# Low-rank token mix after a gated linear recurrence on one Trainium2 core: V r as one float32r product per chunk of stacked halves, and one pair fewer on split weights

## The chip, the cores and the metric

The kernel runs on one core of one Trainium2 chip. The metric is the device time of one execution in microseconds (us); three runs of the kernel before took 533.96, 535.43 and 535.63, a median of 535.43.

A core has engines that run side by side, each through its own queue of instructions in order: PE multiplies matrices (PEld is its loading of weights), DVE and ACT do elementwise work, POOL some of it, and SP issues most of the DMAs. An instruction that waits on a semaphore holds all that is queued behind it on its engine.

## What is computed

Inputs are q, k, v and a complex gate a of shape (4, 8, 768, 48): four batches, eight heads, 768 tokens, 48 columns. The reference first runs a linear recurrence over the tokens of each head, and then a mixer on x of shape (4, 768, 384):

```python
for t in range(S):
    ar, ai = (a_re_n[:, :, t, :, None], a_im_n[:, :, t, :, None])
    new_re = ar * S_re - ai * S_im
    new_im = ar * S_im + ai * S_re
    kv = np.einsum('bhd,bhe->bhde', k[:, :, t], v[:, :, t])
    S_re, S_im = (new_re + kv, new_im)
    y[:, :, t] = np.einsum('bhd,bhde->bhe', q[:, :, t], S_re)
...
    xt = x.transpose(0, 2, 1)
    h = xt @ U @ V
    u = x + h.transpose(0, 2, 1)
    ch = np.maximum(u @ w_ch1, 0.0) @ w_ch2
    return (u + ch).astype(np.float32)
```

Here a_re_n, a_im_n is the gate with its magnitude limited to 0.999. U is 768x32, V 32x768, w_ch1 (w1 below) 384x1536 and w_ch2 (w2) 1536x384. The product x^T U, here called r, is 384x32 in each batch; V r below is what is added to x.

## The kernel before

**Tiles and stages.** The tokens of a batch are six chunks of 128. For each group of two chunks, `gates` makes the decay factors on DVE, ACT and PE; `prep` and `chain` compute the chunk's recurrence with matrix products on PE and leave the chunk's 128x384 of x in a tile `xo`. Two chunks make a pair: three pairs to a batch, twelve in all, numbered 0 to 11. `mixer(m)` does the channel part of pair m:

- `rank` (L1003), once in each batch when its last chunk is there: U^T x for all six chunks, summed in one bank. Four groups of 32 partitions hold r's 32 rows for four column groups, 96 columns each, so r is a tile of 128x96. ACT copies it to SBUF (L1009).
- `spread` (L1063): V r of the pair in eight float32 products (two chunks by four column groups, 32 rows of contraction each), into four banks.
- `mixed` (L467, 128x192): four additions on DVE give u = x + V r in place of `xo`.
- `turned` (L1082): u is transposed on PE for the next product. For pairs 1 to 11 it is then split: DVE takes the upper bits (low, L1104), ACT makes uh (L1106), DVE the rest ul (L1107) and the sum ud (L1109).
- `cut_weights` (L1124 to L1136), once, in pair 1: the same splitting of w1, in six parts of 128x768. DVE masks (wt, L1124), subtracts (w, L1126) and makes wd (L1130); ACT makes wl (L461) and wh (L1136).
- `up_cut` (L1148, L1150, L1155), pairs 1 to 11: u w1 as three float32r products, uh·wh, ul·wl and ud·wd, 36 of each in a pair, 128x256. ACT takes the first two out of PSUM (L461), and DVE adds the third and applies the relu (h, L1169).
- `up` (L1179): the same as one plain float32 product, 36 in a pair. Pair 0 uses it, before V r is known, on x alone ("ahead"). `ranked` (L1190 to L1200) takes r through w1 and `corrected` (L1214 on PE, h L1220 on DVE) then adds V (r w1) to what `up` made.
- the second product, h w2: `down` plain for pair 0 (L1243, 128x384), `down_two` (L1286, 128x192) for pairs 1 to 8, `down_three` (L1463) for the rest.

**Weights.** `weights` and `single` load w1, U, V and w2 and put each together from the two 32-bit words of a number (loads L602, DVE and ACT L616 to L622 and L467; tiles `stage`, `w`). V lies in SBUF as one tile of 128 partitions, its 32 rows four times, one copy for each column group.

**Order.** Every instruction group is an operation in a plan. A table of numbers, `ORDER`, fixes one common order for all engines; each engine's queue is that order cut to its own operations. Nothing is decided later: an engine takes its next instruction when its semaphores are there. `SPARE` says ahead of which operations PE gets idle products of the identity (53 of them). DMAs are issued on SP in the same order; there are transfers of q, k, v (192 KB, L581 and L583), of the gate (L574), of w2 (`stage`, 768 KB, L602), and for each chunk a small trip through DRAM and back (TD<-es L765, T<-TD L768) that turns a row.

## Time and profile before

| | |
|---|---|
| runs | 533.96, 535.43, 535.63 us; median 535.43 |
| the profiled execution | 535.18 us, its span 533.3 |
| granted TensorE clock | 1.00 |
| V r, L1063 | 8.4 us busy in 192 records |
| cut products L1148, L1150, L1155 | 70.6, 68.5 and 55.2 us busy, 396 records each |
| plain up L1179 | 17.4 us busy in 72 records |
| HBM | 33.60 MB read, 4.76 MB written |

The span runs from the first to the last recorded instruction; 1.9 us of the execution's time lie around it. Busy times of PE count each matmul until its modelled end, so neighbours overlap and the mean of a group is longer than the step from one to the next. A group's row reads: line, engine, operation, out<-in by the names of the tiles, shape, count, then busy us, mean ns of one, and the idle time of the engine just before, with what ended it.

### The profile page before, as it was taken

To read this page: it belongs to the slowest core of one execution; us is meant where nothing else is said; L and a number is where in the kernel's file an instruction comes from. 1 tells how busy PE (TensorE), PEld (TensorE's weight loads), DVE (VectorE), ACT (ScalarE), POOL (GpSimd) and SP (SyncE) were. 2 spreads that over 40 slices of the span, in tenths; PEclk is the share of its full clock that TensorE was granted. 3 is DMA by queue.
4 is the path that set the end of the run, shared out by engine and by line. 5 is a ranking of instruction groups with operands and counts; after the bars stand their busy time and mean duration, and the time that the engine had idled before them with its cause. 6 is when DMAs were issued, how large, how long until landed. Compare 5 with 4: busy or idle time off the path is not lost.

```text
span 533.3 us, 17003 instructions
## 1 busy us (share of the span) xinstructions
PE 511.0 (96%) x7454; PEld 466.5 (87%) x7454; DVE 430.7 (81%) x798; ACT 310.5 (58%) x554; POOL 29.9 (6%) x57
## 2 busy tenths in 40 slices
PE   7789999899999998999999999999999999999996
PEld 7567686469999988999999989999999899999996
DVE  7998999999998976886977866786967758788741
ACT  6879999777587783655568764453475652321000
POOL 1000000000102000011002000011002000000020
PEclk9999999999999999999999999999999999999999
DMA  9996968430254442303217460024104300000011
GB/s 185 206 214 163 225 166 197 87 60 1 39 85 105 92 97 29 61 30 69 45 32 128 79 121 17 16 40 91 31 3 85 62 12 2 1 1 1 0 64 52
DMA packets 150704, 39.92 MB, mean 75 GB/s; under 512 B 145880, under 2 KB 147440, under 8 KB 150624
## 3 DMA queue, kind: packets, MB, share of 16 engines
q1 hardware_dynamic: 148544, 34.63, 33.1%
q0 software_dynamic: 2080, 4.15, 2.3%
q8 instruction: 59, 0.97, 0.8%
q14 instruction: 21, 0.17, 0.1%
HBM read 33.60 MB, written 4.76 MB: 72 GB/s over the span
## 4 chain that ended last, share of the span: by engine, by line
PE 79%; DVE 10%; ACT 6%; issue 2%; DMA 1%; SPq 0%; ACTq 0%; DVEq 0%
PE down L1286 20%; PE up L1148 8%; PE bank L1155 8%; PE up L1150 8%; PE bank L1463 7%; PE bank L910 4%; PE bank L881 4%; PE bank L968 4%; PE bank L930 3%; PE bank L960 3%; PE down L1243 2%; PE up L1179 2%; PE bank L1063 1%; PE bank L814 1%; DMA qk<-in_q_dram 1%
## 5 line engine op out<-in xcount | busy, mean ns | idle before, releaser
L1148 PE MATMUL up<-uh,wh 128*128 128x256 f32 x396 | 70.6, 287 | 0.1
L1150 PE MATMUL up<-ul,wl 128*128 128x256 f32 x396 | 68.5, 281 | 0.3 <-DVE ul L1107 0.3
L461 ACT ACTIVATE h<-up 128x512 f32<-128x512 f32 x60 | 35.2, 594 | 46.8 <-PE up L1150 46.3
L1148 PEld LDWEIGHTS up<-uh,wh 128*128 128x128 f32 x396 | 56.8, 189 | 1.2 <-ACT h L461 0.3
L1150 PEld LDWEIGHTS up<-ul,wl 128*128 128x128 f32 x396 | 56.2, 189 | 0.5 <-DVE ul L1107 0.5
L887 ACT COPY QK<-bank 112x512 f32<-112x512 f32 x96 | 51.2, 590 | 8.8 <-PE bank L881 8.6
L1155 PE MATMUL bank<-ud,wd 128*128 128x256 f32 x396 | 55.2, 283 | 0.0
L1286 PE MATMUL down<-w,h 128*128 128x192 f32 x288 | 53.6, 331 | 0.2
L1155 PEld LDWEIGHTS bank<-ud,wd 128*128 128x128 f32 x396 | 50.7, 188 | 0.2
L464 DVE TENSOR_TENSOR QKC<-qk,cs 128x768 f32<-128x768 f32 x48 | 44.9, 955 | 5.8 <-ACT cs L461 4.0
L1286 PEld LDWEIGHTS down<-w,h 128*128 128x128 f32 x288 | 46.6, 190 | 1.5 <-DVE h L1169 0.4
L467 DVE TENSOR_TENSOR xo<-bank,xo 128x192 f32<-128x192 f32 x78 | 26.1, 354 | 24.3 <-PE bank L1463 17.5
L1169 DVE CUSTOM_DVE_ANT_0 h<-bank,h 128x512 f32<-128x512 f32 x54 | 35.8, 687 | 10.2 <-PE bank L1155 8.1
L1286 PE MATMUL down<-stage 128*128 128x192 f32 x192 | 35.7, 333 | 0.5 <-issue 0.3
L800 POOL DMA_DIRECT2D z<-F x15 | 12.1, 806 | 376.1 <-ACT z L461 102.9
L1286 PEld LDWEIGHTS down<-stage 128*128 128x128 f32 x192 | 31.0, 190 | 1.6 <-issue 0.4
L458 ACT ACT_TABLE_LOAD x24 | 30.8, 1283 | 1.1 <-PEq L1670 0.7
L881 PE MATMUL bank<-ident,QKC 64*112 64x64 f32 x768 | 28.5, 220 | 2.4 <-DVE QKC L464 1.7
L881 PEld LDWEIGHTS bank<-ident,QKC 64*112 64x112 f32 x768 | 24.1, 130 | 7.5 <-issue 2.6
L1106 ACT CAST uh<-low 128x384 fp32r<-128x384 f32 x22 | 11.2, 509 | 31.2 <-DVE low L1104 26.6
L910 PE MATMUL bank<-QK 112*64 112x64 f32 x768 | 27.6, 225 | 0.6 <-ACT QK L887 0.6
L910 PEld LDWEIGHTS bank<-QK 112*64 112x64 f32 x768 | 24.3, 138 | 3.9 <-issue 1.7
(234 smaller groups left out, 1066.4 us busy)
## 6 DMA issues: line engine op xcount, KB each, us to landing
stage<-in_moe_w_ch_dram SPq DMA_DIRECT2D x12, 768.0 KB
qk<-in_q_dram SPq DMA_DIRECT2D x24, 192.0 KB
qk<-in_k_dram SPq DMA_DIRECT2D x24, 192.0 KB
values<-in_v_dram SPq DMA_DIRECT2D x24, 192.0 KB
gate<-in_a_re_dram SPq DMA_DIRECT2D x22, 192.0 KB
gate<-in_a_im_dram SPq DMA_DIRECT2D x22, 192.0 KB
out_dram<-xo POOLq DMA_DIRECT2D x13, 192.0 KB, 3.0
out_dram<-xo POOLq DMA_DIRECT2D x16, 96.0 KB, 3.1
```

The source lines that it names most:

```text
L458: ACT(1.4, rank, lambda: nc.scalar.preload_act_table_set(name), writes=[TABLE])
L461: return nc.scalar.activation(out=o, in_=i, func=f, **kw)
L464: nc.vector.tensor_tensor(out=o, in0=a, in1=b, op=OP.mult)
L881: nc.tensor.transpose(out=get(*ps[r])[0:DQ, h], in_=get(*qkc)[at, h].rearrange("p u d -> p (u d)")[:, 0:DQ], identity=ident[at, at], tile_ ...
L887: nc.scalar.copy(out=get(*QK)[0:DQ, u].rearrange("p (h t) -> p h t", t=CH)[:, :, r * HC:(r + 1) * HC], in_=get(*ps[r])[0:DQ])
L910: nc.tensor.matmul(out=get(*ps0)[r:r + HC, h], lhsT=k_of(h, r, HC), rhs=q_of(h, r, HC), start=True, stop=True, tile_position=(0, r))
L1148: nc.tensor.matmul(out=get(*X)[:, e], lhsT=get("wh", f)[:, at(e)], rhs=get(*uh)[:, f], start=(f == 0), stop=False)
L1150: nc.tensor.matmul(out=get(*X)[:, e], lhsT=wl_of(f)[:, at(e)], rhs=get(*ul)[:, f], start=False, stop=(f == KD - 1))
L1155: nc.tensor.matmul(out=get(*Y)[:, e], lhsT=wd[:, f, at(e)], rhs=get(*ud)[:, f], start=(f == 0), stop=(f == KD - 1))
L1169: DVE(c_dve(2 * N), R0, lambda: nc.vector._custom_dve(dve_ops.TENSOR_ADD_SAT, out=where_(), in0=get(*Y), in1=where_(), s0=math.inf, s1=0.0 ...
L1286: nc.tensor.matmul(out=get(*to)[:, part], lhsT=x(j), rhs=y[:, j], start=(first and j == 0), stop=(j == KH - 1), skip_group_check=not first)
L1463: nc.tensor.matmul(out=get(*ps), lhsT=w[0]()[:, q], rhs=x[0]()[:, q], start=(n == 0 and q == 0), stop=(q == k3 - 1), skip_group_check=True)
```

## The change

1. **Pair 1 goes plain.** A new number CUTS = 2 says from which pair on the up product is split. Pair 1 uses `up` (L1179, 36 more float32 products, ACT applies the relu), and u is copied, not split. `cut_weights` is called in pair 2.
2. **V r from stacked halves.** V4 holds V's four copies in float32r: rounded by ACT, and in the second and fourth group of 32 partitions the remainder V − rounded V (two subtractions on DVE). R4, 128x384, holds r's 32 rows four times: rounded in the first and second group, the remainder in the third and fourth. So the four combinations of upper and lower halves are summed by one product 128x384 with 128 rows of contraction: one for each chunk, 24 in all, instead of eight for each pair. `mixed` adds two tiles of 128x384 instead of four of 128x192.
3. **How R4 comes about.** r (128x96, now kept in the first columns of `prefix_z`) is written to DRAM (RD) by a DMA on SP and loaded back into `low`, four times 32x384. In batch 0, where column groups interleave, these are 12 DMAs of 32x4x32; in batches 1 to 3, with another grouping of columns (`thirds_of`), four of 32x4x96. ACT rounds `low` into R4, and DVE subtracts in the lower 64 partitions.
4. **Storage.** The last third of wd shares a buffer with V, which is free once pair 0's corrections are done; QKC lies without gaps; five constants share a tile. w1's two parts get their names by EDGES, with the same borders.
5. **Order.** ORDER and SPARE are new tables; the idle products are 79 instead of 53, the added ones ahead of early operations.

```diff
     PLAIN = 1
     THREE = 9
-    SINGLE, AHEAD = 3, 1
+    SINGLE, AHEAD, CUTS = 3, 1, 2
...
-    wd = singles.tile([128, KD, FF], FR, name="wd")
+    wd = singles.tile([128, KD - 1, FF], FR, name="wd")
+    buffer(("V", 0), "last", 1, [128, S], padded=[128, FF])
+    buffer(("wdx", 0), "last", 1, [128, FF], dtype=FR)
+
+    def wd_of(f):
+        return wd[:, f] if f < KD - 1 else get("wdx", 0)
...
-    V = singles.tile([128, S], FP, name="V")
...
+    V4 = singles.tile([128, S], FR, name="V4")
+    R4 = singles.tile([128, DM], FR, name="R4")
...
+                    ACT(c_act(S), ("w1", p), lambda: nc.scalar.copy(out=V4, in_=get("V", 0)), [("V", 0)], [("V4", 0)])
+                    for n in range(1, NP, 2):
+                        at = slice(n * R, (n + 1) * R)
+                        DVE(c_dve(S), ("w1", p), lambda at=at: nc.vector.tensor_tensor(
+                            out=V4[at], in0=get("V", 0)[at], in1=V4[at].bitcast(FP), op=OP.subtract), [("V", 0)], [("V4", 0, at.start)])
...
-            buffer(r, "r", 1, [128, RC])
+            ring(r, "r", [prefix_z[:, 0:RC]])
...
-                                         rhs=quarter_of(get("xo", b * NCH + c), n), start=(c == 0), stop=(c == NCH - 1),
+                                         rhs=(thirds_of if b else quarter_of)(get("xo", b * NCH + c), n), start=(c == 0), stop=(c == NCH - 1),
...
-            ACT(c_act(RC), R0, lambda: nc.scalar.copy(out=get(*r), in_=get(*sums_r)), [sums_r], [r])
+            ACT(c_act(RC), R0, lambda: nc.scalar.copy(out=get(*r), in_=get(*sums_r)), [sums_r], [r] + [("prefix_z", 0)] * (b == 0))
+            rd = ("RD", b)
+            buffer(rd, "RD", 2, [128, RC], bass.MemoryType.DRAM)
+            SP(0.3, ("load", 7), lambda: nc.sync.dma_start(out=get(*rd), in_=get(*r)), [r], [rd])
+            for n in range(NP):
+                def spread_r(n=n):
+                    x = get(*rd).rearrange("(n r) c -> r n c", r=R)
+                    o = low[n * R:(n + 1) * R]
+                    if b:
+                        nc.sync.dma_start(out=o.rearrange("r (n c) -> r n c", n=NP), in_=x)
+                    else:
+                        for f in range(KD):
+                            nc.sync.dma_start(out=o[:, f * 128:(f + 1) * 128].rearrange("r (n t) -> r n t", t=R), in_=x[:, :, f * R:(f + 1) * R])
+                SP(0.3, ("load", 7), spread_r, [rd], [("low", 0, n)])
+            ACT(c_act(DM), R0, lambda: nc.scalar.copy(out=R4, in_=low), [("low", 0)], [("R4", 0)])
+            DVE(c_dve(DM), R0, lambda: nc.vector.tensor_tensor(
+                out=R4[2 * R:], in0=low[2 * R:], in1=R4[2 * R:].bitcast(FP), op=OP.subtract), [("low", 0)], [("R4", 0)])
...
-                if m == AHEAD:
+                if m == CUTS:
...
-            ps = [out_of("mixed", (m, n), [128, MC, RC], [128, 512 // RC // MC * MC, RC]) for n in range(NP)]
-
-            def products():
-                for cc in range(MC):
-                    for n in range(NP):
-                        at, c = slice(n * R, (n + 1) * R), c0 + cc
-                        nc.tensor.matmul(out=get(*ps[n])[:, cc], lhsT=V[at, c * CH:(c + 1) * CH],
-                                         rhs=get(*r)[at], start=True, stop=True, tile_position=(n * R, 0))
-            PE(0.45, R0, products, [r, ("V", 0)], ps, way=4, steps=4 * NP)
+            ps = [out_of("mixed", (m, cc), [128, DM], [128, 512]) for cc in range(MC)]
+            for cc in range(MC):
+                at = slice((c0 + cc) * CH, (c0 + cc + 1) * CH)
+                PE(0.18, R0, lambda cc=cc, at=at: nc.tensor.matmul(out=get(*ps[cc]), lhsT=V4[:, at], rhs=R4, start=True, stop=True),
+                   [("R4", 0), ("V4", 0)], [ps[cc]], steps=1)
             return ps
 
-        def mixed(n, ps):
-            u = XO[i0 // MC % len(XO)].rearrange("p c (f n t) -> p n c f t", n=NP, t=R)[:, n]
-            DVE(c_dve(MC * RC), R0, lambda: add(u, get(*ps)[:, 0:MC].rearrange("p c (f t) -> p c f t", t=R), u), [ps],
-                [("xo", i0 + cc) for cc in range(MC)])
+        def mixed(cc, ps):
+            DVE(c_dve(DM), R0, lambda: add(get("xo", i0 + cc), get(*ps), get("xo", i0 + cc)), [ps], [("xo", i0 + cc)])
...
-            if ahead:
+            if m < CUTS:
                 for r in range(2):
                     def keep(copy, r=r):
...
-        if m >= AHEAD:
-            if m == AHEAD:
+        if AHEAD <= m < CUTS:
+            for ff in range(0, KF, 2):
+                up(ff)
+        if m >= CUTS:
+            if m == CUTS:
                 cut_weights()
             for ff in range(0, KF, 2):
                 up_cut(ff)

```

The remaining edits rename what point 4 says. The first lines of the tables (the numbers count operations of two different plans):

```diff
-    92, 113, 95, 114, 115, 94, 116, 117, 2206, 0, 93, 97, 91, 3, 96, 118, 4, 98, 99, 102, 103, 104, 119, 105, 106, 120, 121, 107, 108, 110, 112, 111,
+    95, 2202, 98, 97, 116, 117, 118, 119, 120, 121, 96, 94, 193, 0, 5, 151, 99, 100, 122, 123, 101, 102, 105, 106, 107, 103, 108, 109, 3, 124, 110, 4,
```

Three places of the new order, with the lines of the kernel that each row stands in (before and after count lines apart: L1027 is the rank product after, L1100 the new V r product, L1211 up, L1229 the product of r and w1, L1247 corrected, L1253 its sum, L1276 down).

PE, before, from the rank product of batch 0 (up is a piece of pair 0's up product, bank_62<-r,V the first of the eight V r products):

```order
L1003 MATMUL rank<-xo_134,UV 32x96 x8
L1179 MATMUL up<-uT,w_138 128x256
L1179 MATMUL up<-uT,w_139 128x256
L1179 MATMUL up<-uT,w_140 128x256
L1063 MATMUL bank_62<-r,V 128x96
```

PE, after, at the first V r product (the rank product stands some twenty rows ahead of these; R_102 is R4, V_101 is V4, bank_63<-GS and zs belong to the gates of a later group):

```order
L1247 MATMUL bank_66<-V,stage 128x256
L1247 MATMUL bank_61<-V,stage 128x256
L1276 MATMUL down<-w_99,h 128x384 x6
L1100 MATMUL bank_62<-R_102,V_101 128x384
L834 MATMUL bank_63<-GS_115,prefix_r 128x384
L834 MATMUL bank_63<-zs_1419,prefix_r 128x384
L1276 MATMUL down<-w_99,h 128x384 x4
L1100 MATMUL bank_64<-R_102,V_101 128x384
```

Before, V r follows the rank product with one piece of up between; after, it stands behind the corrections and the first six down products.

DVE, before, at the sums of the corrections (w_138 and w_139 are parts of w1, wt the cut):

```order
L467 TENSOR_TENSOR xo_133<-bank_65,xo_133 128x6x32
L622 TENSOR_SCALAR w_96<-w_96 128x768
L1126 TENSOR_TENSOR w_138<-w_138,wt 128x768 x2
L1126 TENSOR_TENSOR w_139<-w_139,wt 128x768
L1220 ISA h<-bank_63,h 128x256
L1220 ISA h<-bank_65,h 128x2x256
L808 CAST GS_115<-z 128x384
L1220 ISA h<-bank_66,h 128x2x256
L1220 ISA h<-bank_61,h 128x2x256
```

DVE, after, at the same sums (F, stage, GS and w_99 belong to gates and weights, R_102<-low,R_102 is R4's subtraction):

```order
L1253 ISA h<-bank_64,h 128x2x256
L1253 ISA h<-bank_65,h 128x2x256
L1253 ISA h<-bank_62,h 128x256
L634 TENSOR_SCALAR w_99<-w_99 128x768
L1048 TENSOR_TENSOR R_102<-low,R_102 64x384
L1253 ISA h<-bank_66,h 128x256
L828 CAST GS_115<-z 128x384
L829 TENSOR_TENSOR zs_1419<-z,GS_115 128x384
L634 TENSOR_SCALAR w_99<-w_99 128x768
```

The cuts of w1 (L1126 before) are gone from here; the subtraction for R4 stands between the sums.

SP, after, around r's write in batch 0 (prefix_z holds r; gate, qk and stage are loads from the inputs):

```order
L586 DMA gate<-in_a_im_dram 128x8x48
L593 DMA qk<-in_k_dram 128x8x48
L1036 DMA RD<-prefix_z 128x96
L614 DMA stage<-in_moe_w_ch_dram 128x2x768
L1045 DMA low<-RD 32x4x32 x3
L586 DMA gate<-in_a_im_dram 128x8x48
L1045 DMA low<-RD 32x4x32 x3
L586 DMA gate<-in_a_re_dram 128x8x48
L785 DMA TD<-es 1x384
L1045 DMA low<-RD 32x4x32 x6
L595 DMA values<-in_v_dram 128x8x48 x2
```

The write and the loads of r take their turns among the loads of the inputs; before there is no transfer of r.

## The prediction

> **What bounds the kernel now.** I read the page first, for the engines and for the chain that ended last.

> ```profile
> span 533.3 us, 17003 instructions
> PE 511.0 (96%) x7454; PEld 466.5 (87%) x7454; DVE 430.7 (81%) x798; ACT 310.5 (58%) x554; POOL 29.9 (6%) x57
> PE 79%; DVE 10%; ACT 6%; issue 2%; DMA 1%; SPq 0%; ACTq 0%; DVEq 0%
> ```

> PE is busy for 96% of the span and carries 79% of the chain; the 10% on DVE must lie somewhere. The windows (busy us of PE, PEld, DVE, ACT, POOL in a stretch, then the granted clock, the DMA share and GB/s) say where:

> ```profile
> 0.00:10.00 10.00, 8.19 (x58) 8.00 (x58) 7.13 (x23) 4.83 (x9) 1.68 (x13) 1.00 0.87 191
> 90.00:100.00 10.00, 6.97 (x42) 3.65 (x39) 10.00 (x19) 9.60 (x14) 0.79 (x1) 1.00 0.99 199
> 100.00:140.00 40.00, 39.38 (x321) 31.52 (x320) 39.60 (x68) 25.29 (x40) 1.68 (x3) 1.00 0.15 26
> 204.00:500.00 296.00, 294.04 (x4216) 281.95 (x4209) 228.49 (x425) 148.94 (x275) 18.66 (x29) 1.00 0.22 42
> ```

> From 204 to 500 us PE lacks 1.96 us of 296: there only PE work counts. From 90 to 140 us DVE has 0.4 us of slack in 50, and PE loses 3.03 us in one slice, 90 to 100, where the DMA engines also stand at 0.99. The chain of waits (start, us, what) through that place:

> ```profile
> 84.83 0.37 PE rank L1003 x8
> 85.20 1.49 PE up L1179 x6
> 86.70 0.67 PE bank L1063 x16
> ...
> 87.62 0.55 DVE wt L1124
> ...
> 90.80 2.60 DVE w L1126 x3
> 93.40 0.93 DVE h L1220 x2
> ...
> 98.17 0.70 PE bank L1214 x4
> ```

> The rank product of batch 0 ends at 85.2, V r follows at 86.7, and DVE cuts w1 (L1124, L1126) before it comes to the corrected h (L1220) for which PE waits. These are PE's longest waits from 84 to 116 us (in all, times, longest):

> ```profile
> PE bank L1214 <- DVE h L1220: 1.4, 1, 1.4
> PE down L1243 <- DVE h L1220: 1.1, 1, 1.1
> ```

> **The change, part by part: PE work.** Paces come from unbroken pieces of the chain, where start to start is what counts. A float32 matmul leaves two records, so L1179 x12 is six matmuls and L1063 x16 eight.

> ```profile
> 63.81 2.59 PE up L1179 x12
> ...
> 103.77 2.58 PE down L1243 x8
> 106.35 0.35 PE bank L814 x2
> ...
> 109.28 0.56 PE bank L1082 x12
> ...
> 205.05 0.25 ACT r L1009
> ...
> 205.34 0.70 PE bank L1063 x16
> 206.04 0.55 PE bank L814 x2
> ...
> 208.09 0.63 PE bank L1063 x16
> ...
> 242.60 0.72 PE bank L1155 x6
> ```

> A plain up product takes 2.59/6 = 0.432 us, a cut product 0.72/6 = 0.12. Pair 1 trades 3×36 cut products (108×0.12 = 13.0 us) for 36 plain ones (15.5 us): **+2.5**. V r costs 0.63 a pair, 7.6 us over 12 pairs. The nearest rows to one float32r product of 128x384 are L814's, of the same shape on float32r data, at 0.175 or 0.275 a piece: 24 make 4.2 to 6.6 us, a saving of 1.0 to 3.4. I take 0.2, nearer the quick pair, which stands between down products as most of the new ones do: **−2.8**. PE work comes out at −0.3, bounds −0.9 and +1.5. The added idle matmuls of the first 10 us go into its 1.8 us without work: 0; without that cover, 26 of them at the 0.43 us of the larger up product would be 11 us at most, but PE has nothing else queued there.

> **DVE.** Rows of its groups (busy, mean ns). Back to back, a duration holds 0.09 us that the next one overlaps (L464 gives 0.955, and L1126 of the same size 2.60/3 = 0.87 on the chain above).

> ```profile
> L467 DVE TENSOR_TENSOR xo<-bank,xo 128x192 f32<-128x192 f32 x78 | 26.1, 354 | 24.3 <-PE bank L1463 17.5 <-PE bank L1063 4.6 <-issue 2.1
> L1169 DVE CUSTOM_DVE_ANT_0 h<-bank,h 128x512 f32<-128x512 f32 x54 | 35.8, 687 | 10.2 <-PE bank L1155 8.1 <-ACT h L461 1.2 <-ACT cs L461 0.8
> L1104 DVE TENSOR_SCALAR low<-bank 128x384 uint32<-128x384 uint32 x22 | 12.2, 555 | 7.0 <-ACT uh L1106 4.5 <-PE bank L1082 2.6
> L464 DVE TENSOR_TENSOR QKC<-qk,cs 128x768 f32<-128x768 f32 x48 | 44.9, 955 | 5.8 <-ACT cs L461 4.0 <-PE bank L881 1.7
> ```

> The sums that add V r to x go from four of 128x192 to two of 128x384 (L1104's size): 4×0.26−2×0.47 = 0.1 us a pair, hidden where PE alone counts. Pair 1 loses six h sums (6×0.60) and the cutting of u (two low and two ul of 0.47, one ud of 0.86): 6.3 us. The cuts of w1 move behind L1220: 0.55+2.60 = 3.15 us leave the stretch of the chain above, while two subtractions for V4 (768 long, so 0.87 each by L464) and one for R4 (384 long, 0.47) come in: L1220 could start 3.15−1.74 = 1.4 us earlier, and end some 3 us earlier where two cuts (L1130, of L464's size) stood between its last instructions. That can give at most PE's 3.03 us of 90 to 100.

> **The exchange.** Where V r waited for one copy by ACT, r now goes to DRAM and back before R4 exists. No row of before has such a trip. These stand nearest: the longest transfer on the chain, a small one of POOL's queue (median to landing), and SP's longest wait for the small write of its own DRAM trip:

> ```profile
> 53.07 5.71 DMA qk<-in_q_dram
> ```

> ```profile
> z<-F POOLq DMA_DIRECT2D x15, 1.5 KB, 1.9
> ```

> ```profile
> SPq L768 <- DMA TD<-es: 7.5, 5, 2.8
> ```

> and SP's issues around this place (start, us):

> ```profile
> 87.32 0.37 SPq L602 DMA_DIRECT2D stage<-in_moe_w_ch_dram  x1
> 87.73 0.73 SPq L581 DMA_DIRECT2D qk<-in_q_dram  x1
> ...
> 89.13 3.15 SPq L574 DMA_DIRECT2D gate<-in_a_im_dram  x1
> ```

> A landing takes 1.9 to 5.7 us. For batch 0 SP's order holds the write of r, then a load of w2 of 768 KB, then the twelve spreading transfers with two gate loads and one TD among them. r is copied at about 85.5; written, it lands by 88.4 (0.4 to issue, 2.5 to land). One stage issue and thirteen small ones at 0.37 with two loads at 0.73 are 6.6 us, so the last issue ends at 95.0 if none is held up; the issue at 89.13 took 2.8 us over the shorter stage one, and I add half of that, 96.4. Then 2.5 to land, ACT's rounding 0.5 and DVE's subtraction 0.5: R4 is ready at **T = 100**. Bounds: 97.5 (nothing held up, landings of 1.9) and 107 (2.8 more, landings of 5.7).

> Who waits: DVE has R4's subtraction in the midst of the L1220 sums and stops there, with all that is queued behind it (two L1220 sums, the sums of V r, gates, the cuts). From the rank's end DVE has four instructions of 0.87, six L1220 (four of 0.60 and two about half as long) and seven of about 0.47 ahead of it, 9.8 us: it arrives near 95.4 and stands some 4 us. PE comes to V r after six down products of 0.645 (2.58 for four): with the corrections done by about 96, where before they ended at 98.9, it arrives at 96+3.9 = 99.9. At T = 100 PE loses nothing, and every us beyond is one of PE's. Behind V r lie 18 down products (11.6 us), three more V r (0.6), the sum on DVE (0.5), the turning of u (L1082, 0.56) and its copy (1.0 for two halves), so pair 1's up would start at about 114.3, against these (PE's timeline):

> ```profile
> 115.90 0.62 PE L1148 MATMUL up<-uh,wh 128*128 128x256 f32 x3
> ...
> 148.50 0.65 PE L1148 MATMUL up<-uh,wh 128*128 128x256 f32 x3
> ```

> That is up to −1.6 of idle time. But DVE, 6.3 us lighter and held up for 4, still has all the cuts of w1 (6×(0.47+2×0.87) = 13.3 us, part of which it had done by then before) ahead of pair 2's up, 148.5 in before. I keep **−0.5**.

> [...]

> **Batches 1 to 3.** Four spreading transfers take the place of twelve. Before, V r waited for ACT's copy from 205.05 to 205.34, 0.3 us, in batch 1. Now 24, 24 and 27 down products of 128x192, half of 0.645 each by their size, stand behind the rank product: 7.7 to 8.7 us. The exchange: copy 0.25, issue 0.4, landing 2.5, four issues 1.5, landing 2.5, rounding and subtraction 1.0, together 8.2; bounds 7.0 and 14.6. So up to 0.5 us in each is exposed, less the 0.3: **+0.5** together.

> **The sum.** −0.3−0.5+0.5 = −0.3 on the profiled execution's 535.18 us (the span of 533.3 and 1.9 around it), so 534.9. That execution is 0.25 us under the median of 535.43: the forecast is **535.0**, and no change beyond 0.3%, 1.6 us, about what a measurement of this kernel can tell from none.

> **The rivals.**

> *Late exchange (slower).* The twelve transfers stand in SP's queue behind the large load and on engines at 0.99. DVE stops in order at R4's subtraction, PE right behind it at V r; from T = 100 on, each us costs one. With one held-up issue in full (1.4 more) and one landing of 4.6, two thirds of the way from 2.5 to 5.7 (2.1 more), T = 103.5: −0.3+3.5 = +3.2, 538.4. For it: the 0.99 and the issue of 3.15 us. Against: each transfer is 16 KB. 0.27.

> *Early exchange (faster).* With T at 97.5, DVE's shorter way to L1220 is kept and PE's 3.03 us shrink to about 0.3: −0.3−2.7 = −3.0, 531.9. For it: 1.9 us of z<-F. Against: SP's sixteen issues, which alone are 6.6 us. 0.22.

> *DVE's lighter stretch pays.* DVE bounds 100 to 140 (39.60 of 40); if the 6.3 us gone from pair 1 are worth 4 there in spite of the cuts that moved, 530.9. Against: the cuts still come before pair 2's up. 0.10.

> *Exchange exposed in each batch (slower).* At the bound of 14.6 us, 6.4 us of each exchange would show; at a quarter of that way, 1.6 each, three batches cost 4.9: 539.5. The DMA share of 0.22 from 204 us on speaks against it. 0.06.

> *The change doesn't do what it says:* products of 0.275 us make PE work +1.5 instead of −0.3, 536.7, just at the bound of no change; it is part of the forecast's share.

> **How the numbers follow.** Forecast 0.35, of it 0.28 within 0.3%, 0.04 faster, 0.03 slower; its own range is 533.3 to 536.7. Faster: 0.04+0.22+0.10 = 0.36. Slower: 0.03+0.27+0.06 = 0.36. Same: 0.28. The range reaches into the rivals on both sides and leaves out about a tenth on each: 531.0 to 539.3.

> **What would show it.** In the profile after: R4's subtraction (L1048) of batch 0 ending between 99 and 101, with some 4 us of idle DVE ahead of it; under 1 us of wait at the first V r product (L1100), and pieces of it at 0.18 to 0.28 us; pair 1's up starting near 114.3 and lasting 15.5; waits of PE under 1 us at V r in batches 1 to 3. I am wrong if L1048 ends after 102 or before 98, if V r of a later batch holds PE for over 2 us, or if PE's idle time between 100 and 160 us changes by more than 2 us.

## The result and the profile after

The changed kernel takes **530.8 us** (median of 16 runs, 529.88 to 533.72) against 535.63 (median of 16, 533.35 to 540.69) for the kernel before on the same chip: a ratio of 0.9907 with a 95% interval of 0.9882 to 0.9931, so some 0.9% faster. It lies 0.2 us below the lower end of the predicted range and 4.2 us below the predicted time. The profiled execution took 530.23 us, 4.95 less than the one of before.

The page of the changed kernel, first its span, its engines and the chain that ended last:

```profile
span 528.1 us, 16716 instructions
PE 515.3 (98%) x7302; PEld 472.0 (89%) x7302; DVE 429.7 (81%) x770; ACT 312.1 (59%) x558; POOL 29.7 (6%) x57
PE 76%; ACT 8%; DVE 6%; SPq 4%; DMA 3%; issue 2%; DVEq 0%; ACTq 0%
```

PE's busy time rose by 4.3 us although the span fell by 5.2 us. The windows of the changed kernel (busy us of PE, PEld, DVE, ACT, POOL, then clock, DMA share and GB/s) say where the idle time went:

```profile
0.00:10.00 10.00, 8.60 (x55) 8.60 (x56) 7.37 (x24) 4.72 (x8) 1.71 (x13) 1.00 0.92 197
90.00:100.00 10.00, 8.89 (x41) 5.22 (x40) 7.84 (x17) 7.20 (x9) 0.96 (x1) 1.00 0.70 146
160.00:204.00 44.00, 43.54 (x947) 40.81 (x947) 36.50 (x61) 30.03 (x60) 2.24 (x4) 1.00 0.45 84
204.00:500.00 296.00, 295.08 (x4079) 284.46 (x4078) 232.93 (x422) 149.44 (x276) 17.11 (x27) 1.00 0.22 43
```

and of the kernel before, a stretch that the prediction did not look at:

```profile
160.00:204.00 44.00, 42.32 (x938) 39.23 (x938) 37.17 (x65) 33.34 (x64) 3.24 (x5) 1.00 0.51 98
```

PE's idle time fell from 3.03 to 1.11 us between 90 and 100, from 1.68 to 0.46 between 160 and 204, and from 1.96 to 0.92 between 204 and 500. The first of these falls is in the exchange that the prediction worked out, the other two are not.

The exchange of batch 0 is on the chain of waits of the changed kernel (start, us, what):

```profile
85.47 0.25 ACT prefix_z L1033
...
88.97 4.68 DMA gate<-in_a_im_dram
...
95.49 0.43 SPq L1045
...
95.96 1.79 DMA low<-RD
...
97.86 0.52 ACT R L1047
...
98.40 0.56 DVE R L1048
```

r is copied at 85.5, SP's last spreading transfer is issued at 96.0, lands 1.8 us later, and R4 is ready at 98.96. The timelines of DVE and of PE show what that cost (idle before, releaser in brackets):

```profile
98.40 0.56 DVE L1048 TENSOR_TENSOR R<-low,R 64x384 fp32r<-64x384 f32 x1 [2.06 <-ACT R L1047]
```

```profile
99.01 0.45 PE L1100 MATMUL bank<-R,V 128*128 128x384 f32 x1 [0.83 <-DVE R L1048]
```

The price of the work around pair 1, again from the chain:

```profile
104.81 0.35 PE bank L1100 x2
...
114.68 7.77 PE up L1211 x36
```

Two records of V r take 0.35 us, 0.175 for each product, and 36 records of the plain up product 7.77 us, or 0.432 for each of the 18 products of this piece. The later exchanges are hidden; batch 1's, which waits longest:

```profile
196.46 0.25 ACT prefix_z L1033
...
201.84 1.99 DMA low<-RD
203.90 0.52 ACT R L1047
204.44 0.57 DVE R L1048
205.05 0.62 PE bank L1100 x2
```

Pair by pair (us from the span's start, PE's timeline), the lead grows late:

| | before | after | difference |
|---|---|---|---|
| rank product of batch 0 ends | 85.2 | 85.1 | −0.1 |
| pair 1's up starts | 115.9 | 114.5 | −1.4 |
| pair 3's cut up starts | 210.6 | 209.8 | −0.8 |
| pair 6's cut up starts | 329.9 | 327.1 | −2.8 |
| pair 9's cut up starts | 448.6 | 442.2 | −6.4 |
| PE's last product ends | 528.7 | 523.2 | −5.5 |

The exchange gives 1.4 us. Some 4 us more come after 210, where the prediction had nothing.

**What the late gain is made of.** PE's waits that no other engine ends, in the kernel before and then after (in all, times, longest):

```profile
PE bank L960 <- issue: 2.9, 4, 1.0
PE bank L968 <- issue: 0.4, 1, 0.4
PE bank L930 <- issue: 0.4, 1, 0.4
PE down L1286 <- issue: 0.3, 1, 0.3
PE bank L881 <- issue: 0.3, 1, 0.3
```

```profile
PE bank L934 <- issue: 0.5, 1, 0.5
```

4.3 us against 0.5; of the eight pieces before, three lie ahead of 140 us. On the timeline of before such a standstill looks like this, in the midst of a run of one line's small products whose data are there:

```profile
200.71 0.37 PE L960 MATMUL bank<-values,AT 64*64 64x48 f32 x9
202.12 0.56 PE L960 MATMUL bank<-values,AT 64*64 64x48 f32 x23 [1.04 <-issue]
```

The page of before has a queue that carries instructions (packets, MB, share of 16 engines), and so has that of after:

```profile
q8 instruction: 59, 0.97, 0.8%
```

These are packets of 16 KB. In the kernel before PE runs 14,963 instructions (14,660 after), if weight loads, matmuls and its semaphore waits are counted in order of time from 0: 58 blocks of 256, so about one packet for each. All of PE's late standstills lie at the same place in a block, and all end at nearly the same distance from the landing of a packet:

```
PE's instruction        its remainder  starts   after the one    last packet  that far
                        by 256         at us    ahead of it, us  landed at    behind it
before  5824            192            197.57   0.57             196.28       1.30
before  6080            192            202.12   1.25             200.58       1.54
before  7616            192            265.06   0.52             263.74       1.32
before  9664            192            317.29   0.60             315.81       1.48
before  12480           192            422.66   1.10             421.23       1.44
after   5824            192            191.89   0.68             190.51       1.38
```

The rivals: the gain comes from the late **order**, which was arranged anew, or from **DVE**, which has two sums for a pair where it had four. For the exchange there is one more: the trip's time sets pair 1's start one for one (theory T) or is hidden anyway.

### The profile page after: what moved, and what is told of

It reads as the page before. It is cut to its first block, busy times and chain, and to the rows that moved or that the text cites. A ratio compares the mean times of both kernels' runs of the same rounds, so it can differ in the third digit from the quotient of the medians.

```text
span 528.1 us, 16716 instructions
## 1 busy us (share of the span) xinstructions
PE 515.3 (98%) x7302; PEld 472.0 (89%) x7302; DVE 429.7 (81%) x770; ACT 312.1 (59%) x558; POOL 29.7 (6%) x57
## 3 DMA queue, kind: packets, MB, share of 16 engines
HBM read 34.38 MB, written 4.95 MB: 74 GB/s over the span
## 4 chain that ended last, share of the span: by engine, by line
PE 76%; ACT 8%; DVE 6%; SPq 4%; DMA 3%; issue 2%; DVEq 0%; ACTq 0%
PE down L1319 18%; PE up L1182 8%; PE bank L1189 8%; PE up L1184 7%; PE bank L1496 7%; PE bank L905 4%; PE bank L934 4%; PE up L1211 4%; PE bank L992 3%; PE bank L954 3%; PE down L1276 2%; PE bank L984 2%; ACT QK L911 2%; PE bank L834 1%; PE bank L770 1%
## 5 line engine op out<-in xcount | busy, mean ns | idle before, releaser
L1182 PE MATMUL up<-uh,wh 128*128 128x256 f32 x360 | 64.7, 288 | 0.4 <-DVE xo L467 0.4
L1184 PE MATMUL up<-ul,wl 128*128 128x256 f32 x360 | 62.1, 281 | 0.0
L911 ACT COPY QK<-bank 112x512 f32<-112x512 f32 x96 | 52.0, 591 | 11.6 <-PE bank L905 7.5
L461 ACT ACTIVATE h<-up 128x512 f32<-128x512 f32 x60 | 35.5, 595 | 30.9 <-PE up L1184 28.8
L1182 PEld LDWEIGHTS up<-uh,wh 128*128 128x128 f32 x360 | 51.5, 189 | 2.0 <-ACT cs L461 0.5
L464 DVE TENSOR_TENSOR QKC<-qk,cs 128x768 f32<-128x768 f32 x48 | 45.0, 953 | 6.9 <-ACT cs L461 5.7
L1189 PE MATMUL bank<-ud,wd 128*128 128x256 f32 x240 | 45.1, 283 | 0.0
L467 DVE TENSOR_TENSOR xo<-bank,xo 128x192 f32<-128x192 f32 (+1 forms) x54 | 22.8, 440 | 18.4 <-PE bank L1496 17.2
L1189 PEld LDWEIGHTS bank<-ud,wd 128*128 128x128 f32 x240 | 37.0, 188 | 0.1
L1189 PE MATMUL bank<-ud,wdx 128*128 128x256 f32 x120 | 33.7, 281 | 0.0
L1211 PE MATMUL up<-uT,w 128*128 128x256 f32 x144 | 33.6, 384 | 0.0
L1211 PEld LDWEIGHTS up<-uT,w 128*128 128x128 f32 x144 | 26.7, 190 | 4.7 <-issue 0.6
L467 DVE TENSOR_TENSOR xo<-down,xo 128x192 f32<-128x192 f32 (+1 forms) x58 | 22.1, 384 | 10.7 <-PE down L1319 10.5
L1140 ACT CAST uh<-low 128x384 fp32r<-128x384 f32 x20 | 10.2, 512 | 33.7 <-DVE low L1138 28.3
```

Of the source, the lines that this page charges most:

```text
L461: return nc.scalar.activation(out=o, in_=i, func=f, **kw)
L464: nc.vector.tensor_tensor(out=o, in0=a, in1=b, op=OP.mult)
L467: nc.vector.tensor_tensor(out=o, in0=a, in1=b, op=OP.add)
L911: nc.scalar.copy(out=get(*QK)[0:DQ, u].rearrange("p (h t) -> p h t", t=CH)[:, :, r * HC:(r + 1) * HC], in_=get(*ps[r])[0:DQ])
L1182: nc.tensor.matmul(out=get(*X)[:, e], lhsT=get("wh", f)[:, at(e)], rhs=get(*uh)[:, f], start=(f == 0), stop=False)
L1184: nc.tensor.matmul(out=get(*X)[:, e], lhsT=wl_of(f)[:, at(e)], rhs=get(*ul)[:, f], start=False, stop=(f == KD - 1))
```

## The experiments

A ratio is to the kernel before, measured beside the run, with its 95% interval. The first four ask for the whole of the late gain: by the place of the borders, by the order, by the products.

**e1_shift.** Nine idle products of the first 30 us in small pieces, so that every later instruction stands 128 places further on.

```diff
+        late = calls.count(n) - 6
+        if n == SHIFT_AT and late > 0:
+            for _ in range(5 if late <= 5 else 4):
+                nc.tensor.matmul(out=to[:, 0:1] if len(to.shape) == 2 else to[:, 0, 0:1], lhsT=ident, rhs=ident[:, 0:1], start=True, stop=True)
+            return
```

> The kernel after, with PE's instruction stream moved by 128 instructions: early on, where PE is idle anyway, nine idle products are replaced by 41 of one column, and nothing else is touched. Theory A (PE's instructions come in blocks of 256, and PE stands still at a block's border when the block before it was run through faster than the next one came; the order of after spreads the small products of the recurrence so that few borders are reached early): the pauses called issue come back at other places, at borders that now lie 128 instructions elsewhere in the program; 12 blocks then run in under 4 us instead of 7, and the time goes up by 1.5 to 5 us, to 532.3 to 536. Theory B (the gain comes from DVE, which has less to do in pair 1 and per pair): no change, 530.8 within 0.5.

548.37 us, ratio 1.022 [1.0198, 1.0242]. Both sizes were missed, for a cost that was in neither. PE's timeline and the window of 30 to 40 us:

```profile
25.96 14.46 PE L1657 MATMUL bank<-ident 128*128 128x1 f32 x82
```

```profile
30.00:40.00 10.00, 10.00 (x48) 10.00 (x49) 0.00 (x0) 0.65 (x1) 0.00 (x0) 0.50 0.15 58
```

82 records of one column take 14.5 us, and the granted clock falls to 0.50. The rank product ends at 102.9 instead of 85.1, which is the loss. From there on the kernel takes 1.7 us more than the changed one, of it 0.4 in late pauses (1.08 against 0.68). Two more pauses at block borders stand behind the rank product here, 1.70 us at 104.3 and 0.32 at 132.0, the first of them PE's longest wait:

```profile
PE up L1213 <- issue: 1.5, 1, 1.5
```

Behind it the clock is at 0.50 for 3.4 us. On the other side PE no longer waits for R4. So the shift does bring pauses, but early ones, and for the late gain the run doesn't decide.

**e2_late_order_before** and **e3_late_order_after.** The common order from pair 2's cut up on, exchanged between the two kernels; in ORDER the first numbers that differ are:

```diff
-    544, 501, 513, 556, 555, 744, 558, 783, 496, 739
+    544, 501, 513, 2194, 550, 551, 496, 675, 674, 566
```

```diff
-    773, 539, 540, 566, 567, 743, 745, 744, 774, 541
+    773, 539, 540, 334, 649, 650, 433, 813, 815, 732
```

> The kernel after up to the first cut up product of pair 2, and from there the order of before (the operations that only after has stay behind the operation that they follow on their engine). Edits and work as in after. Theory A (the order of the recurrence's small products among the large ones is what saved time late): slower than after by 2.5 to 5 us, 533.3 to 536. Theory B (the edits save it): as after, 530.8 within 1.

> The kernel before (V r of eight products for each pair, pair 1 cut) up to the first cut up product of pair 2, and from there the order of after. Theory A: faster than before by 2.5 to 5 us, 530.5 to 533. Theory B: as before, 535.4 within 1.

565.45 us, ratio 1.0541 [1.0518, 1.0565], and 558.61, ratio 1.0409 [1.0386, 1.0431]: both theories were missed by 20 us and more, with a granted clock of 0.976 and 0.977 in the profiled executions. Neither tells anything of the question; it seems that an order fits its own products. The longest of PE's waits in e2 and in e3:

```profile
PE bank L1105 <- DVE R L1053: 14.1, 4, 5.1
```

```profile
PE bank L818 <- DVE GS L812: 4.2, 1, 4.2
```

In e2, V r stands where no exchange was allowed for and waits 14.1 us.

**e4_old_vr.** The changed kernel with V r as eight float32 products of a pair, in the changed order.

```diff
-            ps = [out_of("mixed", (m, cc), [128, DM], [128, 512]) for cc in range(MC)]
-            for cc in range(MC):
...
+            ps = [out_of("mixed", (m, n), [128, MC, RC], [128, 512 // RC // MC * MC, RC]) for n in range(NP)]
+
+            def products():
+                for cc in range(MC):
+                    for n in range(NP):
...
```

> The kernel after with V r as it was before (eight float32 products for each pair from one tile of V, no trip of r through DRAM, no V4 and R4), pair 1 plain, in the order of after; the storage is that of before. Theory A: PE has 1.8 us more work (12 times 0.63 against 24 times 0.24) and loses the 1.1 us of waits for R4, so 530.8 + 0.7 = 531.5, between 530.5 and 533. Theory B (the product per chunk and its fewer sums are the gain): most of the 4.8 us come back, 534 to 535.5.

558.46 us, ratio 1.041 [1.0382, 1.0438]. Inconclusive too: four banks and four sums for a pair seem not to fit an order made for two. PE waits 3.4 us in two waits at one line alone, a small part of the loss; the rest was not followed up:

```profile
PE bank L1175 <- DVE xo L471: 3.4, 2, 2.2
```

**e5_after_124** and **e6_before_52.** The stream shifted without a change of what follows: the first idle products of each kernel in pieces of 32 columns (124 instructions more in the changed kernel, 52 in the one before). The second has the same edit with 4 and 5 for 10 and 11.

```diff
+        calls.append(n)
+        parts = 4 if len(calls) <= 10 else 2 if len(calls) <= 11 else 1
...
-            nc.tensor.matmul(out=to[:, 0:CH], lhsT=ident, rhs=ident, start=True, stop=True)
+            for x in range(0, CH, CH // parts):
+                nc.tensor.matmul(out=to[:, x:x + CH // parts], lhsT=ident, rhs=ident[:, x:x + CH // parts], start=True, stop=True)
```

> The kernel after with PE's stream moved by 124 instructions without taking idle work away: of the first idle products of the program ten are split into four of 32 columns and one into two of 64. By the trace of after, with the borders of the blocks of 256 instructions there, blocks of under 4.2 us after 140 us would lack 13.5 us in sum instead of 4.5. Theory A (pauses at blocks' borders): they come back, 2 to 5 us in sum after 140 us at the granted clock of 1.00, and the time is 532.5 to 535.5. Theory B (the edits are the gain, the borders cost nothing): 530.8 within 0.6.

> The kernel before with PE's stream moved by 52 instructions in the same way (four of the first idle products in four, one in two). By the trace of before the blocks under 4.2 us after 140 us would lack 7.7 us in sum instead of 11.3, and those under 3.2 us 0.5 instead of 2.2. Theory A: the pauses of 4.0 us after 140 us shrink by 1 to 3 us, and the time with them: 532.5 to 534.5. Theory B: no change, 535.4 within 0.6.

The 4.2 and 3.2 us under which these expectations count a block are limits that the author chose for the sums; in the trace of before eight blocks of 2.5 to 4.2 us after 140 us end without a pause. e5: 546.81 us, ratio 1.0194 [1.0168, 1.022]. e6: 539.84, ratio 1.0061 [1.0029, 1.0093]. The totals again hold an early cost (the rank product ends 15.5 us late in e5 and 6.1 in e6), which PE's timeline of e5 shows:

```profile
2.70 17.84 PE L1655 MATMUL warm<-ident 128*128 128x32 f32 x82
```

The late part of e5 in the same view, at 420 us:

```profile
419.55 0.44 PE L954 MATMUL bank<-values,QKC 64*48 64x48 f32 x21
421.82 0.38 PE L954 MATMUL bank<-values,QKC 64*48 64x48 f32 x11 [1.83 <-issue]
```

With the same late stream, but for the borders and for loads that have 15 us more lead, the changed kernel gets three late pauses, 0.60, 2.04 and 0.88 us (3.52 in all, against 0.68), and the stretch from pair 6's to pair 9's cut up takes 118.1 us instead of 115.1. In e6 the late pauses of before fall from 4.04 to 2.65 and the time from the rank product to PE's last falls by 1.4. So a shift of the same stream moves the late part by one to three microseconds, in either direction, with the pauses.

**e7_trip_first.** All of batch 0's loads of r ahead of the 768 KB load of w2 on SP. Four operations change place in ORDER:

```diff
-    421, 409, 79, 413, 651, 411, 649, 631, 412, 410, 700
+    421, 409, 410, 411, 412, 413, 79, 651, 649, 631, 700
```

> The kernel after with the twelve loads of r in batch 0 ahead of the 768 KB load of w2, the two gate loads and the TD write on SP; all else as in after. R4 would be ready about 2.5 us earlier, near 96.5. Theory T (as forecast: PE comes to V r when R4 is ready, and is held by it): PE's waits of 0.83 for R4 and 0.43 behind it go, the time falls by 0.5 to 1.3 us. Rival (what the trip holds up is not on the path to the end): within 0.4 of after. A second rival (the loads that are pushed back by 5 us are late for the gates): 0.5 to 2 us more.

534.07 us, ratio 0.9973 [0.9953, 0.9992], 0.66% of the kernel before, or 3.5 us, more than the changed kernel. The load now starts 6 us later, and DVE needs it for the product behind the corrections (timelines of DVE and PE):

```profile
98.05 0.61 DVE L637 TENSOR_SCALAR stage<-stage 128x768 uint16<-128x768 uint16 x1 [4.09 <-DMA stage<-in_moe_w_ch_dram]
```

```profile
99.29 5.49 PE L1281 MATMUL down<-w,h 128*128 128x384 f32 x8 [3.54 <-DVE h L1258]
104.00 1.09 PE L1105 MATMUL bank<-R,V 128*128 128x384 f32 x1
```

The wait changed its name, from r to w2. It is not the whole of the 3.5 us: in this execution (535.89 us) the granted clock also stands at 0.50 for 6.8 us from 98.2, which the 1.09 us of the V r product show; the two runs of e7 with a clock of 0.999 and more took 532.57 and 533.34. T is not tested by this, since R4 came no earlier (its subtraction ends at 101.2).

**e8_dve_more.** 36 instructions of DVE on 160 columns added to the changed kernel, behind the sums of pairs 3 to 11.

```diff
+                if m >= 3:
+                    for x in (0, 192):
+                        nc.vector.tensor_scalar(out=spill, in0=get("xo", i0 + cc)[:, x:x + 160], scalar1=2.0, scalar2=None, op0=OP.mult)
...
```

> The kernel after with 36 more instructions on DVE, two of 160 columns behind each sum of V r from pair 3 on (some 0.25 us each, 9 us in sum, three times what the change takes from DVE in those pairs); their result is not used. Theory A (DVE's relief in batches 1 to 3 is worth nothing): 530.8 to 531.8. Theory B (the relief is the gain): 533 or more.

537.59 us, ratio 1.0035 [1.0018, 1.0051], by the ratios 6.9 more than the changed kernel. The longest of PE's waits at up:

```profile
PE up L1188 <- DVE xo L467: 1.3, 3, 0.9
```

PE's waits that the sums (xo) end at up, at the turning of u and at down are 3.4 us in all (the first two were 0.6 in the changed kernel). So more of DVE costs much, in part because it stands between V r and the turned u, on which up waits; the rest of the 6.9 us was not traced.

**e9_fewer_sums.** The other way round: the kernel before, with two of a pair's four sums cut to one column in 32.

```diff
+            w = R if m < 3 or n < 2 else 1
...
```

> The kernel before, where from pair 3 on two of the four sums that add V r to x take one column in 32 (the rest of V r is left out of u there): 18 instructions of 128x192 are cut from 0.26 to about 0.1 us, 3 us less on DVE in batches 1 to 3, on the way from V r to the turning of u. Theory B (DVE's time per pair is what holds PE in batches 1 to 3; the run with 9 us more on DVE was 6.8 us slower): 1.5 to 3 us faster than before. Theory A (pauses at blocks' borders and the order are the gain; the sums had room in before): within 0.8 of before.

534.63 us, ratio 0.9999 [0.9973, 1.0025]. Lighter sums in the later pairs are worth nothing that shows to the kernel before (the interval reaches some 1.4 us either way): DVE's relief there, the second rival, falls as the source of the late gain. The pauses are at the same borders as in before (196.5, 200.8, 263.7 and 420.7 us; the one at 317.3 is gone), for the stream of PE is the same.

**e10_53_idle.** The changed kernel with 53 idle products, as many as before.

```diff
-    113: 12, 136: 9, 140: 2, 204: 15, 206: 15, 225: 1, 241: 2, 250: 7, 267: 1, 274: 2, 2202: 13,
+    113: 12, 136: 9, 140: 2, 204: 6, 206: 4, 225: 1, 241: 2, 250: 1, 267: 1, 274: 2, 2202: 13,
```

> The kernel after with 53 idle products, as many as before had, instead of 79 (26 fewer between 18 and 30 us); PE's stream moves back by 104 instructions, which by the trace of after would make the blocks under 4.2 us after 140 us lack some 10 us instead of 4.5. Forecast's view (the added idle products fill idle time: 0): 530.8, and 1 to 3 more for pauses at other borders. Rival (they keep the clock up; without them it is halved for some us, as where 41 products of one column stood): 4 to 13 us slower, with a granted clock below 1.00 between 20 and 60 us.

537.59 us, ratio 1.0051 [1.0024, 1.0077]: 7.7 more than the changed kernel by the ratios, 6.9 between the profiled executions. The clock falls to 0.83 between 20 and 30 us, and PE's waits have these:

```profile
PE bank L959 <- DVE QKC L469: 2.6, 1, 2.6
PE bank L989 <- issue: 2.5, 1, 2.5
PE rank L1032 <- issue: 1.7, 1, 1.7
PE bank L939 <- issue: 1.5, 1, 1.5
```

The rank product ends 7.9 us late; behind it, the time is that of the changed kernel less 1.1. The size is the one that the rival named, and the clock does fall (0.50 for 3.4 us from 23.3 and again from 40.4). But the three waits on issue are pauses at block borders, at 39.9, 86.0 and 91.8 us, 6.3 us from start to start, where the changed kernel has none: taking the products out has moved the borders by 104 instructions too. The run doesn't tell the two apart. The added idle products buy nothing against the kernel before, since the rank product ends at the same time in both; that the new early order needs them for the clock is not shown.

**e11_trip_on_two_queues.** Half of batch 0's loads of r on POOL's queue.

```diff
-                            nc.sync.dma_start(out=o[:, f * 128:(f + 1) * 128].rearrange("r (n t) -> r n t", t=R), in_=x[:, :, f * R:(f + 1) * R])
+                            (nc.gpsimd if n >= 2 else nc.sync).dma_start(out=o[:, f * 128:(f + 1) * 128].rearrange("r (n t) -> r n t", t=R), in_=x[:, :, f * R:(f + 1) * R])
...
```

> The kernel after with the trip of r in batch 0 split over two queues: six of the twelve loads are issued by POOL, idle there, and six stay on SP. SP's last load would go out some 2.6 us earlier. Theory T: R4 ready at 97 instead of 98.96, PE's 1.3 us of waits around V r go, 529.5 to 530.3. Rival (POOL's issues are slow, 0.8 us each, or the transfer z<-F behind them is late for the gates): as after or up to 3 us slower.

**529.36 us**, ratio 0.9879 [0.9848, 0.9911], the fastest kernel here, though its interval overlaps that of the changed kernel. Its chain and PE's timeline:

```profile
88.81 5.69 DMA low<-RD
...
97.51 0.52 ACT R L1050
...
98.06 0.56 DVE R L1051
```

```profile
98.67 0.44 PE L1103 MATMUL bank<-R,V 128*128 128x384 f32 x1 [0.33 <-DVE R L1051]
```

R4 is ready 0.35 us earlier, pair 1's up starts 0.35 earlier, at 114.15, and PE's wait goes from 0.83 to 0.33. That speaks for T, one for one, for as long as PE still waits at V r; 0.33 is left to gain. But R4 was expected at 97 and came at 98.62: SP's last load of r was issued at 93.0 instead of 96.0, more than planned, and most of that was lost on the way: the chain has a load of r that landed after 5.69 us (the last one of the changed kernel took 1.79), and ACT waited for a landing until 97.5.

**e12_whole_rows.** The kernel before, with q, k and v from chunk 8 on read in whole rows.

```diff
+    def whole(a, i):
+        flat = a.rearrange("b h t d -> (b h t d)")[i * CH * DM:(i + 1) * CH * DM]
+        return rows(a, i) if i < 8 else flat.rearrange("(p h d) -> p h d", h=H, d=D)
...
```

> The kernel before, where from chunk 8 on q, k and v are loaded from 192 KB of the input that lie together (128 pieces of 1536 bytes) instead of 1024 pieces of 192 bytes each, so that u is not that of the reference from chunk 8 on; the order and all instructions of the engines are those of before. If the blocks of PE's instructions are late because they share the DMA engines with such loads: the late pauses at the borders (4.0 us after 140 us in the profile of before, at 197.6, 202.1, 265.1, 317.3 and 422.7) shrink to under 1.5 us and the time falls by 2 to 3 us. Rival (how fast the block before was run through decides alone): the pauses and the time stay, within 0.8 of before.

533.7 us, ratio 0.9975 [0.995, 1.000]. The late pauses are 1.81 us instead of 4.04 (0.82 at 202.6, 0.99 at 317.8), in the same stream of PE: the other three places lost theirs to 0.18 at most. The time is 0.25% less, and the interval ends at none. Lighter loads may have a part in how late a block comes, but e9 lost one of the five pauses without them and two stay here, so one run doesn't settle it.

**The account.** From the end of batch 0's rank product to PE's last product:

| run | us | late pauses | without them |
|---|---|---|---|
| before | 443.5 | 4.04 | 439.5 |
| e9, before with fewer sums | 442.3 | 2.80 | 439.5 |
| e6, before shifted by 52 | 442.1 | 2.65 | 439.5 |
| e12, before with whole rows | 443.1 | 1.81 | 441.3 |
| after | 438.1 | 0.68 | 437.4 |
| e11, r on two queues | 437.4 | 0.84 | 436.6 |
| e10, after with 53 idle | 437.0 | 1.46 | 435.5 |
| e5, after shifted by 124 | 439.7 | 3.52 | 436.2 |
| e1, after shifted by 128 | 439.8 | 1.08 | 438.7 |

In the kernel before, the pauses add one for one: without them three runs agree to 0.1 us, and the fourth, e12, has a dip of the clock of some 1.7 us (last section).

For the changed kernel the table leaves out what lies between the rank product and 140 us: 1.28 us of pause at 102.1 in e5, and in e1 the pauses of 1.70 and 0.32 and 1.7 us lost to the clock. Without these e5 comes to 434.9 and e1 to 435.0. The runs of the changed kernel then come to 434.9 to 437.4, 2.1 to 4.6 us less than before. The three lowest, e10, e5 and e1, have a rank product that is 8 to 18 us late, and PE doesn't wait for R4 there; after's waits for it are 1.1 us, e11's less, so that explains a part of what is between them.

So between the two profiled executions 3.4 us of the 5.4 are pauses and 2.0 are the rest. How an average run divides is open, because the pauses of one stream vary: the profiles of before's stream (before, e9) have 4.04 and 2.80, and e12's with lighter loads 1.81; those of after's (after, e7, e8, e11) have 0.68, 1.54, 0.95 and 0.84. That is 2.4 us between the means, without e12.

## Why the prediction was wrong

The change did what it says, and the working held for the exchange. The faster side was given 0.36, for reasons that were only partly the right ones.

- *PE work −0.3.* Plain up at 0.432 us a product, 15.5 in all, was right: +2.5. V r was forecast at 0.2 us and took 0.175: 4.2 us instead of 7.6, −3.4 and not −2.8.
- *Idle products at 0.* Right against the kernel before, where the rank product ends at 85.2 and after at 85.1. The trace doesn't show why: before has 1.84 us of pauses at block borders ahead of the rank product (39.2, 70.4 and 75.1 us), the changed kernel none, so the 0 may hold two things that cancel. That taking them out of the changed kernel would cost 7 us (e10) was not seen; the bound of 11 was for their price, not for their use.
- *R4 at T = 100, DVE standing some 4 us, PE at V r at 99.9.* R4 came at 98.96, DVE stood 2.06 us, PE arrived at 98.2 and waited 0.83. SP's last issue ended at 96.39, and 96.4 was worked out for it: in part luck, for the first load of r went out at 87.6 instead of 88.8, and the issues took longer than assumed, with a gate transfer of 4.68 us among them on the chain. The last load landed 1.4 us after that end, where 2.5 was allowed, and that is the 1 us by which R4 came early.
- *Pair 1's up at 114.3, of the gain −0.5 kept.* It came at 114.5, and all of the 1.4 us was kept: PE's idle time between 100 and 160 us fell from 0.69 to 0.38. The fear for DVE's cuts ahead of pair 2's up had no ground.
- *Batches 1 to 3, +0.5.* PE's waits for R4 are 1.1 us in all, 0.8 of them batch 0's. The remaining 0.3 is as much as V r waited for ACT's copy before: 0.
- *The rivals.* Neither the late nor the exposed exchange came. The early exchange has the right place (PE's idle time of 90 to 100 fell to 1.11), at half of the price it was given. DVE's lighter stretch hit the time, 530.9, by luck, through a mechanism that isn't there: e9 gives DVE's relief in the later pairs no worth, and 100 to 160 us gave 0.3. Two of the times are 0.3 off their own terms: −3.0 on 535.18 is 532.2 and not 531.9, and −0.3 and 4.9 make 539.8 and not 539.5; nothing hangs on it.

With the measured sizes the forecast's own terms make +2.5 −3.4 −1.4 = −2.3. But the 1.4 hold 0.85 us that the 3.4 count already: batch 0's V r, three times 0.63 before and six times 0.175 after, lies ahead of pair 1's up. So it is some −1.5, near the rest of −2.0 in the account but not equal to it.

**The step that failed** is "From 204 to 500 us PE lacks 1.96 us of 296: there only PE work counts". The 1.96 us were read as nothing. They were in the main pauses at block borders (at 265.1, 317.3 and 422.7 us), as was most of the 1.68 between 160 and 204, and the change moved the borders: the sum had no term for PE's standstills, which gave 3.4 of the 5.4 us between the two profiled executions. The chain's "issue 2%" was quoted and not followed up. It would not have told it either, for it is 2% after as well. The waits ended by "issue" would have, 4.3 us in eight pieces. None of the signs that the prediction named for being wrong came up (L1048 ended at 98.96, between 98 and 102; the idle time of 100 to 160 changed by 0.3): it looked for its errors only where it had worked. What the sum needed was a term of −4 to 0 for them: most of what the stream of before loses to pauses can go when instructions are added or removed, and come back with a shift (e5).

Shown are the place of the pauses, their tie to the instruction packets, and that they add one for one in the stream of before. That a stream's pauses depend on where the borders fall follows from e5 and e6, whose late streams are the same but for that (and that their loads have more lead). Not settled is how much of the gain in pauses comes from the borders' new places and how much from the new late order, since e2 and e3 failed as a test.

## What to carry to other kernels

On an engine that is busy for 96% and more, look at its waits ended by "issue" before calling the rest idle time, and count its instructions: here the standstills that recurred at one remainder by 256, each 1.29 to 1.64 us behind the landing of an instruction packet, were its program coming late in bursts of small instructions. Instructions added ahead of such bursts moved these pauses (3.52 us of late ones in e5 against 0.68 in the changed kernel, 2.65 in e6 against 4.04 in the one before), so a gain of under 1% may be where the borders fall; a shift of the same stream tells it apart, if the padding itself is cheap. The trip through DRAM was paid for by its issues and by the wait in the queue (in the changed kernel from 85.7 to 96.4 us on SP, 4.68 of it a gate transfer on the chain): splitting the issues over two queues helped a little (e11, 0.35 us for issues that ended 3 us earlier), moving the trip ahead of a large load only gave the wait another name (e7, 4.09 us of DVE for w2).

## What the chip showed beside it

- **Small products were not cheap.** With 128x128 weights, a record of 1 column took 0.18 us (14.46 us for 82 in e1) and one of 32 columns 0.22 (17.84 for 82 in e5). In e1 the granted clock was 0.50 between 30 and 40 us, with PE busy for 10.00 of 10.
- **Idle time alone didn't tell when the clock falls.** In e12 PE was busy for 2.41 of 4 us from 94 to 98, and the clock went down to 0.68 and 0.50 for the next 4 us, at a cost of some 1.7 us (an estimate from the clock from 98 to 104; windows of 2 us):

```profile
94.00:96.00 2.00, 1.55 (x5) 0.79 (x5) 2.00 (x5) 2.00 (x4) 0.00 (x0) 1.00 1.29 186
96.00:98.00 2.00, 0.86 (x3) 0.19 (x1) 2.00 (x4) 2.00 (x4) 0.00 (x0) 1.00 1.35 188
98.00:100.00 2.00, 1.78 (x6) 1.05 (x7) 2.00 (x5) 2.00 (x3) 0.73 (x1) 0.68 0.71 101
100.00:102.00 2.00, 2.00 (x4) 1.09 (x4) 2.00 (x6) 1.12 (x2) 0.23 (x1) 0.50 0.02 1
```

  In the kernel before PE was busy for 2.41 of the same 4 us as well, with the same waits, and the clock stayed at 1.00:

```profile
94.00:96.00 2.00, 1.60 (x5) 0.79 (x5) 2.00 (x5) 2.00 (x4) 0.00 (x0) 1.00 1.01 194
96.00:98.00 2.00, 0.81 (x3) 0.19 (x1) 2.00 (x4) 2.00 (x4) 0.00 (x0) 1.00 1.18 201
98.00:100.00 2.00, 1.82 (x8) 1.10 (x9) 2.00 (x5) 2.00 (x3) 0.79 (x1) 1.00 0.71 105
```

  What decides it, these runs don't show.

- **Much of the spread between runs goes with the clock.** Over the 75 runs of the kernel before that stand beside the experiments, the time follows the mean granted clock: 533.86 us at 1.000 and 0.52 us more for each 0.001 below it (correlation −0.79). The gain does not come from there: at a clock of 0.999 and more, which 28 of those 75 runs and 6 of the changed kernel's 16 have, the medians are 534.1 and 530.6 us.
